# A new order for all elementwise instructions of a fused attention and two-layer kernel

## The chip, the cores and the metric

The kernel runs on one core of a Trainium2 chip. The metric is device time in microseconds (us), the median of several executions. Six queues matter here. PE is the matrix engine (PEld its weight loads), DVE is VectorE, ACT is ScalarE, POOL is GpSimd, and SP issues DMAs. Each engine works through its own instructions strictly in the order in which they were written, and waits on semaphores for what other engines have yet to deliver.

## The reference

Attention with a hash mask (a query sees only keys that fall into the same one of 64 buckets), then two feed-forward layers; the first uses mish, the second elu.

```
mask = q_bucket[:, :, :, None] == k_bucket[:, :, None, :]      # buckets: signs of q @ proj, k @ proj
scores = where(mask, scale * q @ k^T, -1e9)                    # 2 x 8 heads, 768 x 768, head size 64
attn = exp(scores - max) / (sum + 1e-9);  out = attn @ v
x = out as (1536, 512)
h = x @ w_in;  x = (h * tanh(softplus(h))) @ w_out             # 512 -> 2048 -> 512
h = x @ w_in2; x = where(h > 0, h, exp(h) - 1) @ w_out2        # 512 -> 2048 -> 512
```

Inputs are float32. Every factor is split into a rounded high part and a low part (names ending in hi and lo), and a product is the sum of three matmuls.

## The kernel before

**Attention** (to about 233 us). 16 heads of 6 query tiles each give 96 tiles. For a tile, PE computes scores `st` (L648), DVE takes the maximum while it copies them to `pt` (L651, L654), ACT does the exponential (L656). For a pair of tiles PE transposes `pt` into `tu` (L707, three pieces), ACT writes the high part `pth` (L712), DVE the low part `ptl` (L353, called from the split), and PE multiplies both with the values (`xt`, L720). There are two `tu` buffers, so a late `ptl` holds up the next transpose. POOL splits the inputs (`z`, `vt`) and divides and splits the finished heads (`xr`, L757, L761, then `x_hi` and `x_lo`).

**Weights.** 64 units of 128x512 float64 numbers come in by DMA and are turned into two float32 parts by `convert`, nine instructions each on ACT, DVE and POOL. The first three units are converted between the attention tiles; the DVE steps of these read and write SBUF alone (L405, L410, L413, L415, L418, with `wt` and `ws`). Later units keep one operand, `c`, in PSUM. Units 6 and 7, 10 and 11 and so on are pairs for which POOL also forms sums `sa` and `sb`.

**The two layers** (from about 233 us). `up` products give `h`, one per unit and column block; mish or elu makes `g` of it; `down` products of `g` are summed in `y_acc`. Pairs of units run as seven products with shared sums (a Strassen scheme, `pair_step`); for that `turn` forms differences of x first (`y_acc` as scratch, L1040, split into `T`), once before each layer's pairs. The last step of elu is the subtraction `g<-gg,g` (L353 through `elu`). It and the steps of `turn` may run on DVE or on POOL.

**What sets the order.** `Plan` collects all operations with their costs and dependencies, and `Plan.run` walks a simulated clock: for each engine it takes the waiting operation with the lowest priority number among those that can start soon, and of all engines the earliest start. That order is then emitted. Where an operation may run on DVE or POOL, the plan also decides which. In the plan, POOL and DVE operations marked `port` never overlap. The priority is the place in the program plus tables: `OFF` and `ODD` for attention (by kind of operation, and by kind and tile of the head), `SHIFT` for weights and layers. In the two layers PE's own order is fixed by the program; in attention PE's order comes from the tables too. `pool(n)` and `pool2(n)` are the plan's costs in ns for a POOL instruction over n columns.

Of the kernel before, what the change touches and what calls it, by code (L numbers as in the profile page):

```python
# [30 lines left out]
def unit_orders():  # L31
# [25 lines left out]
EDGE = {}  # L57
SHIFT = {
# [86 lines left out]
def pool(n):  # L145
    return 150 + 2.22 * n


def pool2(n):
    return 150 + 2.38 * n  # L150
# [144 lines left out]
def kernel(ctx, tc, qk, v, w, tab, out):  # L295
# [165 lines left out]
    def attention(p, ap, dp, pss, pst, psx, h_r):  # L461
# [52 lines left out]
        def order(i, name):  # L514
            return i + OFF[name] + ODD.get(name, (0,) * NQ)[i % NQ] + EDGE.get(f"{name}{i}", 0)

# [784 lines left out]
```

## Time and profile before

| | us |
|---|---|
| median of 3 runs | 739.52 (739.17 to 742.06) |
| profiled execution, its own time | 742.38 |
| its span, first to last instruction | 740.6 |
| PE busy in it | 727.1 |
| DVE, ACT, POOL busy | 579.4, 490.4, 423.2 |

[...] The profile's "idle before" of an instruction is the time its engine stood still just ahead of it, followed by what ended that.

### The profile page before, as it was taken

How to read it: one execution, taken by the hardware profiler on the slowest of the kernel's cores; microseconds unless marked ns; L12 is line 12 of the kernel's file. 1: busy time of each engine (PE TensorE's matmuls, PEld its weight loads, DVE VectorE, ACT ScalarE, POOL GpSimd, SP SyncE). 2: the span in 40 equal slices, each digit the busy share in tenths (PEclk: the TensorE clock that was granted, in tenths of full speed). 3: DMA queues.
4: the chain of work that ended last, by engine and by line, in shares of the span. 5: the costliest groups of instructions: out<-in, count | busy, mean ns of one | idle time of the engine just before them, and what ended most of it. 6: DMA issues, size and time to landing. Idle time of an engine off the chain costs nothing. (4 is left out here: it accounts for less than half of the span.)

```text
span 740.6 us, 11709 instructions
## 1 busy us (share of the span) xinstructions
PE 727.1 (98%) x4083; PEld 639.0 (86%) x4083; DVE 579.4 (78%) x1065; ACT 490.4 (66%) x977; POOL 423.2 (57%) x359
## 2 busy tenths in 40 slices
PE   8999999999999999999999999999999999999998
PEld 7999999999898887888888888887788888888887
DVE  6899999999998979486577668999766785866672
ACT  5998998989997666554273457467766754844740
POOL 5427735734637886446446536866664755765640
PEclk9999999999999999999999999999999999999999
DMA  6875867777620302122112202212121121121112
GB/s 191 206 187 150 204 176 178 190 175 184 143 61 29 114 30 70 44 86 85 58 58 74 98 30 86 86 57 81 34 86 58 58 86 58 58 85 58 58 72 99
DMA packets 27498, 72.93 MB, mean 98 GB/s; under 512 B 6048, under 2 KB 8240, under 8 KB 27440
## 3 DMA queue, kind: packets, MB, share of 16 engines
q1 hardware_dynamic: 27296, 72.17, 34.3%
q8 instruction: 32, 0.52, 0.3%
q14 instruction: 26, 0.21, 0.1%
q10 hardware_dynamic: 144, 0.01, 0.0%
HBM read 45.76 MB, written 3.19 MB: 66 GB/s over the span
## 5 line engine op out<-in xcount | busy, mean ns | idle before, releaser
L848 PE MATMUL h<-g,w 128*128 128x512 f32 x1140 | 267.1, 390 | 3.0 <-DVE g L353 3.0
L848 PEld LDWEIGHTS h<-g,w 128*128 128x128 f32 x1140 | 212.6, 188 | 48.0 <-DVE g L353 4.1
L353 DVE TENSOR_TENSOR ptl<-tu,pth 128x512 fp32r<-128x512 f32 x144 | 97.5, 687 | 7.4 <-ACT pth L712 5.0
L651 DVE TENSOR_SCALAR_CACHE_REDUCE pt<-st 128x768 f32<-128x768 f32 x96 | 90.6, 948 | 5.7 <-PE st L648 5.4
L656 ACT ACTIVATE pt<-pt,nb 128x768 f32<-128x768 f32 x96 | 90.7, 945 | 3.6 <-DVE nb L654 3.4
L712 ACT CAST pth<-tu 128x512 fp32r<-128x512 f32 x144 | 82.2, 582 | 13.6 <-PE tu L707 12.7
L707 PE MATMUL tu<-ident,pt 128*128 128x128 f32 x576 | 85.9, 275 | 2.9 <-DVE ptl L353 2.8
L353 POOL TENSOR_TENSOR wt<-wt,w 128x512 f32<-128x512 f32 x40 | 52.8, 1320 | 62.1 <-DVE c L415 39.4
L1202 DVE TENSOR_TENSOR y_acc<-h,y_acc 128x512 f32<-128x512 f32 x71 | 48.8, 687 | 50.3 <-PE h L848 50.2
L648 PE MATMUL st<-qkt 76*128 76x384 f32 (+1 forms) x384 | 86.7, 350 | 0.8 <-DVE pt L651 0.8
L720 PE MATMUL xt<-pth,vt 128*128 128x256 f32 x288 | 79.3, 304 | 0.0
L707 PEld LDWEIGHTS tu<-ident,pt 128*128 128x128 f32 x576 | 67.4, 140 | 10.4 <-DVE ptl L353 6.2
L720 PE MATMUL xt<-ptl,vt 128*128 128x256 f32 x288 | 72.7, 281 | 0.0
L648 PEld LDWEIGHTS st<-qkt 76*128 76x128 f32 (+1 forms) x384 | 63.8, 191 | 1.7 <-DVE pt L651 1.7
L848 PE MATMUL h<-x_hi,w 128*128 128x512 f32 x192 | 60.5, 390 | 0.0
L348 ACT CAST w<-wt 128x512 fp32r<-128x512 f32 (+1 forms) x64 | 37.2, 583 | 33.0 <-DVE wt L401 18.0
L423 POOL TENSOR_TENSOR wt<-wt,ws 128x512 f32<-128x512 f32 x24 | 31.9, 1328 | 42.5 <-DVE ws L418 42.0
L432 POOL TENSOR_TENSOR w<-wt,ws 128x512 fp32r<-128x512 f32 x40 | 53.4, 1335 | 4.6 <-DVE ws L418 2.2
L720 PEld LDWEIGHTS xt<-ptl,vt 128*128 128x128 f32 x288 | 54.7, 190 | 0.1
L720 PEld LDWEIGHTS xt<-pth,vt 128*128 128x128 f32 x288 | 54.4, 189 | 0.0
L398 DVE TENSOR_SCALAR c<-ws 128x512 int32<-128x512 int32 x61 | 42.0, 689 | 14.3 <-ACT ws L396 12.7
L350 POOL CAST z<-rw 128x768 fp32r<-128x768 f32 x14 | 11.6, 826 | 64.0 <-DMA qkt<-z 41.7
(151 smaller groups left out, 1549.8 us busy)
## 6 DMA issues: line engine op xcount, KB each, us to landing
wraw<-in_w_dram SPq DMA_DIRECT2D x64, 512.0 KB
qkt<-z SPq DMA_DIRECT2D x30, 384.0 KB
rw<-in_qk_dram SPq DMA_DIRECT2D x16, 384.0 KB
qkt<-z SPq DMA_DIRECT2D x31, 192.0 KB
vr<-in_v_dram SPq DMA_DIRECT2D x8, 384.0 KB
out_dram<-y_acc SPq DMA_DIRECT2D x11, 256.0 KB
rr<-dr SPq DMA_DIRECT2D x14, 192.0 KB
xs<-xr SPq DMA_DIRECT2D x14, 192.0 KB
```

The lines of the kernel that those rows point to most:

```text
L348: nc.scalar.copy(out=out, in_=in_)
L353: eng(e).tensor_tensor(out=out, in0=a, in1=b, op=ALU.subtract)
L398: o2 = p.op({DVE: dve(n)}, lambda e: nc.vector.tensor_scalar(out=bits(b), in0=bits(a), scalar1=3, scalar2=None, op0=ALU.logical_shift_left ...
L432: o9 = p.op({POOL: cost}, lambda e: nc.gpsimd.tensor_tensor(out=lo(), in0=t.tile, in1=s.tile, op=ALU.add), [o6, o8], [t, s, w_], prio)
L648: nc.tensor.matmul(st.tile[:, c, 0:HS], lhsT=wt.tile[0:n, q, t * 128:(t + 1) * 128], rhs=wt.tile[0:n, 2 + q, c * HS:(c + 1) * HS], start=( ...
L651: o = max_op = p.op({DVE: dve(S)}, lambda e: nc.vector.tensor_scalar(out=half(pt.tile), in0=st.tile[:, :, 0:HS], scalar1=-MASKED / SCALE, ...
L656: o = p.op({ACT: act(S, False) + 196}, lambda e: nc.scalar.activation(out=pt.tile, in_=pt.tile, func=AF.Exp, bias=nb.tile, scale=SCALE, ac ...
L707: nc.tensor.transpose(tu.tile[:, k, j], pt.tile[:, (2 * b + k) * 128:(2 * b + k + 1) * 128], ident)
L712: o = p.op({ACT: act(512)}, lambda e, tu=tu, ks=ks: nc.scalar.copy(out=hi.tile[:, ks], in_=flat(tu)), [o], [tu, hi], order(i, 'hi'))
L720: nc.tensor.matmul(xt.tile[:, 0:TH], lhsT=vt.tile[:, k, g % 2], rhs=m.tile[:, k], start=(k == 0 and j == 0), stop=(k == NKT - 1 and j == 1))
L848: nc.tensor.matmul(out(), lhsT=w_.tile[:, a, k], rhs=r, start=(start and n == 0), stop=(stop and n == 3 * len(ks) - 1), skip_group_check=True)
L1202: y = p.op({DVE: dve(n)}, lambda e, ya=ya, t=t, c=c: nc.vector.tensor_tensor(out=ya, in0=view(t.tile, c), in1=ya, op=ALU.add), [x, Y[m, c] ...
```

## The change

Only numbers change; no function but the two cost lines does. Both cost lines now say 140 + 2.185 n (1259 ns for 512 columns where they said 1287 and 1369). A third table, `EDGE`, which was empty, now shifts single operations of the first heads (1 to 5) and the last ones (13 to 15). All entries of `OFF`, `ODD` and `SHIFT` are new.

```diff
-EDGE = {}
+EDGE = {'rr5': -12.0, 'rh#1': -1.0, 'rh#2': -4.0, 'rh#3': 3.75, ...
 SHIFT = {
-    'P1#0': -28, 'P1#1': -25.25, 'P1.1': -5, 'P1c#0': -20.5, 'P1c#1': 3.5, 'P1c.1': -22.75, 'P2#0': 19.5,
...
+    'P1#0': -27.25, 'P1#1': -97.5, 'P1.1': 5.75, 'P1c#0': 114.75, 'P1c#1': 8, 'P1c.1': -51, 'P2#0': -17.5,
...
 def pool(n):
-    return 150 + 2.22 * n
+    return 140 + 2.185 * n
 def pool2(n):
-    return 150 + 2.38 * n
+    return 140 + 2.185 * n
```

What it does to the program: all lines of the kernel move down by two (L353 becomes L355). Every computation stays. 11 instructions go from DVE to POOL: 7 of the elu subtractions `g<-gg,g` (DVE 22 to 15, POOL 26 to 33), and of `turn` a net 4. PE's order is unchanged up to 20 us and in both layers; it changes around heads 2 to 4 and 13 to 15. In the middle of attention (heads 6 to 12) nearly all orders stay.

In the first heads, DVE's `wt0` step (L410 before, L412 now) comes ahead of the maximum of tile 23 and of one `ptl17`, three instructions earlier; on POOL the split of `z6` and the addition to `xr0` change places.

DVE, last heads, around `ws1`, a step in the conversion of weight unit 1 (`ptl79`, `ptl81`, `ptl83` are low parts; `pt85` and the like come from the maximum, `both15` is a mask). Before:

```order
L654 TENSOR_SCALAR nb83_3103<-mx83_3015 128x1
L415 TENSOR_SCALAR ws1_2827<-wt1_2872 128x512
L581 SCALAR_TENSOR_TENSOR both15_3096<-pj15_3080,both15_3096 64x384
L353 TENSOR_TENSOR ptl79_3078<-tu79_2_3090,pth79_3060 128x512
L651 TENSOR_SCALAR pt85_3127,mx85_3126<-st85_3098 128x768
```

Now:

```order
L355 TENSOR_TENSOR ptl79_3078<-tu79_1_3067,pth79_3059 128x512
L583 SCALAR_TENSOR_TENSOR both15_3099<-pj15_3080,both15_3099 64x384
L355 TENSOR_TENSOR ptl79_3078<-tu79_2_3091,pth79_3059 128x512
L653 TENSOR_SCALAR pt85_3126,mx85_3125<-st85_3103 128x768
L355 TENSOR_TENSOR ptl81_3144<-tu81_0_3112,pth81_3128 128x512
L653 TENSOR_SCALAR pt84_3155,mx84_3154<-st84_3120 128x768
L355 TENSOR_TENSOR ptl81_3144<-tu81_1_3130,pth81_3128 128x512
L656 TENSOR_SCALAR nb84_3175<-mx84_3154 128x1
L653 TENSOR_SCALAR pt87_3178,mx87_3177<-st87_3147 128x768
L355 TENSOR_TENSOR ptl81_3144<-tu81_2_3158,pth81_3128 128x512
L656 TENSOR_SCALAR nb87_3202<-mx87_3177 128x1
L656 TENSOR_SCALAR nb85_3204<-mx85_3125 128x1
L417 TENSOR_SCALAR ws1_2827<-wt1_2872 128x512
```

`ws1` stood between tiles' work ahead of the last `ptl79`; it now stands behind all of `ptl79` and `ptl81`, some 6 us of DVE work later.

ACT, first layer, around the first pair of units (`p6_01` and `p6_02` are copies of a PSUM bank that the next product waits for; `w8` and `w9` are high parts of weights). Before:

```order
L348 CAST w8_4078<-wt8_4075 128x512
L348 CAST T0_0_3697<-y_acc_3696 128x256
L348 COPY p6_01_4108<-h6_b1_4088 128x512
L348 CAST w9_4110<-wt9_4105 128x512
L348 CAST x_hi_64<-y_acc_3696 128x256
L348 COPY p6_02_4133<-h6_b1_4088 128x512
```

Now:

```order
L350 CAST w8_4104<-wt8_4088 128x512
L350 CAST T2_0_3701<-y_acc_3696 128x256
L350 COPY p6_01_4121<-h6_b1_4096 128x512
L350 CAST w9_4133<-wt9_4123 128x512
L892 ACTIVATE h6_b2_4110<-h6_b2_4110 128x512
L350 COPY p6_02_4146<-h6_b1_4096 128x512
```

The cast of `x_hi` out of `y_acc`, which needs a `turn` step of DVE, no longer stands ahead of `p6_02`. On DVE, the seven instructions that end with the step `wt9` had a `T` subtraction and a `y_acc` subtraction among them; now the steps of `w8` and `w9` follow each other up to `wt9` with none between.

POOL, start of the second layer. `g32` to `g35` are the first four elu outputs (the last figure is the column block), `w36` and `w37` the first `down` weights. Before:

```order
L353 TENSOR_TENSOR wt36_5978<-wt36_5978,w36_5982 128x512
L432 TENSOR_TENSOR w36_5982<-wt36_5978,ws36_5930 128x512
L353 TENSOR_TENSOR wt37_6077<-wt37_6077,w37_6081 128x512
L353 TENSOR_TENSOR g33_2_6102<-gg1217_6063,g33_2_6102 128x512
L353 TENSOR_TENSOR g32_1_6110<-gg1224_6075,g32_1_6110 128x512
L432 TENSOR_TENSOR w37_6081<-wt37_6077,ws37_6053 128x512
```

Now:

```order
L355 TENSOR_TENSOR T2_1_3702<-y_acc_3696,T2_1_3702 128x512
L355 TENSOR_TENSOR g33_2_6080<-gg1217_6051,g33_2_6080 128x512
L355 TENSOR_TENSOR wt36_6082<-wt36_6082,w36_6086 128x512
L434 TENSOR_TENSOR w37_6054<-wt37_6046,ws37_6025 128x512
L434 TENSOR_TENSOR w36_6086<-wt36_6082,ws36_6062 128x512
L1042 TENSOR_TENSOR y_acc_3696<-y_acc_3696 128x256
L355 TENSOR_TENSOR g35_0_6192<-gg1245_6162,g35_0_6192 128x512
L355 TENSOR_TENSOR T2_0_3701<-y_acc_3696,T2_0_3701 128x256
L355 TENSOR_TENSOR g34_2_6203<-gg1252_6186,g34_2_6203 128x512
```

`g35_0`, `g34_2`, `g32_2` and three `T` subtractions were DVE's and are POOL's now, `g32_1` went the other way, and `w36` comes behind `w37`.

## Rows read from the trace of the kernel before

**Rows 1.** The page: engines' busy time; costliest group (mean ns, idle, releaser).

```profile
PE 727.1 (98%) x4083; PEld 639.0 (86%) x4083; DVE 579.4 (78%) x1065; ACT 490.4 (66%) x977; POOL 423.2 (57%) x359
...
L848 PE MATMUL h<-g,w 128*128 128x512 f32 x1140 | 267.1, 390 | 3.0 <-DVE g L353 3.0
```

**Rows 2.** PE's waits, whole span: us in total, times, longest.

```profile
PE h L848 <- DVE g L353: 3.0, 3, 1.4
PE tu L707 <- DVE ptl L353: 2.8, 3, 1.0
...
PE h_b L848 <- ACT p L348: 0.8, 1, 0.8
...
PE st L648 <- DVE pt L651: 0.8, 2, 0.6
```

**Rows 3.** Windows: stretch, length, busy time by engine (instructions), clock, DMA.

```profile
60.00:180.00 120.00, 120.00 (x902) 116.45 (x901) 110.43 (x266) 110.16 (x245) 70.00 (x49) 1.00 0.73 179
...
720.00:741.00 21.00, 17.46 (x89) 14.76 (x87) 5.00 (x8) 0.00 (x0) 0.00 (x0) 1.00 0.28 100
```

**Rows 4.** Timeline at 55 us: start, length, engine, line, names, [idle <-releaser].

```profile
54.88 1.84 POOL L757 TENSOR_TENSOR xr<-xr,xs 128x768 f32<-128x768 f32 x1
...
55.27 2.00 DVE L410 SCALAR_TENSOR_TENSOR wt<-wraw,wt 128x512 int32<-128x512 int32 x1
...
57.93 0.66 PE L707 MATMUL tu<-ident,pt 128*128 128x128 f32 x4 [0.98 <-DVE ptl L353]
```

**Rows 5.** Timeline at 195 us.

```profile
194.47 1.84 POOL L353 TENSOR_TENSOR x_lo<-xr,x_hi 128x768 fp32r<-128x768 f32 x1
...
194.61 1.98 DVE L415 TENSOR_SCALAR ws<-wt 128x512 int32<-128x512 int32 x1
...
197.70 0.55 PE L707 MATMUL tu<-ident,pt 128*128 128x128 f32 x3 [1.04 <-DVE ptl L353]
```

**Rows 6.** Timeline, 280 to 299 us.

```profile
280.39 1.50 DVE L353 TENSOR_TENSOR T<-y_acc,T 128x256 fp32r<-128x256 f32 x1
...
282.52 0.62 ACT L348 CAST w<-wt 128x512 fp32r<-128x512 f32 x1 [2.30 <-DVE wt L401]
...
284.52 0.50 PE L848 MATMUL h_b<-x_hi,wb 128*128 128x512 f32 x1 [0.84 <-ACT p L348]
...
298.87 0.50 PE L848 MATMUL h<-g,w 128*128 128x512 f32 x1 [0.39 <-DVE g L353]
```

**Rows 7.** Timeline, 515 to 527 us.

```profile
515.92 2.36 DVE L353 TENSOR_TENSOR g<-gg,g 128x512 fp32r<-128x512 f32 x2
...
516.08 1.66 POOL L423 TENSOR_TENSOR wt<-wt,ws 128x512 f32<-128x512 f32 x1 [0.84 <-DVE ws L418]
...
518.34 5.75 PE L848 MATMUL h<-g,w 128*128 128x512 f32 x24 [1.29 <-DVE g L353]
...
523.04 2.35 DVE L353 TENSOR_TENSOR g<-gg,g 128x512 fp32r<-128x512 f32 x2
...
525.45 1.90 PE L848 MATMUL h<-g,w 128*128 128x512 f32 x7 [1.36 <-DVE g L353]
```

**Rows 8.** POOL and DVE groups by line and shape: count, busy us, mean ns, idle.

```profile
L353 POOL TENSOR_TENSOR g<-gg,g 128x512 fp32r<-128x512 f32 x26 | 33.5, 1298 | 14.6 <-ACT g L348 14.6
...
L1040 POOL TENSOR_TENSOR y_acc<-x_hi,x_lo 128x512 f32<-128x512 f32 x8 | 11.0, 1389 | 0.4 <-DVE x_lo L353 0.4
...
L1040 POOL TENSOR_TENSOR y_acc<-x_hi,x_lo 128x256 f32<-128x256 f32 x8 | 7.5, 952 | 0.0
...
L353 DVE TENSOR_TENSOR g<-gg,g 128x512 fp32r<-128x512 f32 x22 | 20.6, 954 | 3.1 <-ACT g L348 2.7
...
L353 DVE TENSOR_TENSOR g<-h_b,g 128x512 fp32r<-128x512 f32 x24 | 16.5, 686 | 7.6 <-ACT g L348 7.6
```

**Rows 9.** Timeline, 233 to 245 us.

```profile
233.08 0.47 PE L848 MATMUL h<-x_hi,w 128*128 128x512 f32 x1
...
236.16 0.67 ACT L396 ACTIVATE ws<-wraw 128x512 f32<-128x512 f32 x1
...
243.43 1.31 POOL L432 TENSOR_TENSOR w<-wt,ws 128x512 fp32r<-128x512 f32 x1
```

More of the change, by code (lines that the diff above doesn't have):

```diff
@@ L56 @@
 SEED, SPREAD = 0, 0.0
-EDGE = {}
+EDGE = {'rr5': -12.0, 'rh#1': -1.0, 'rh#2': -4.0, 'rh#3': 3.75, 'rh#13': -10.5, 'rh#14': 31.5, 'cp#1': 5.5, 'cp#3': 1.5, 'cp#14': -5.25, 'cp#15': 19.75, 'ld#1': -16.0, 'ld#2': -11.75, 'ld#13': -4.0, 'ld#14': 19.0, 'ld#15': 14.5, 'sp#1': -27.0, 'sp#2': -1.25, 'sp#13': -7.5, 'sp#14': -15.5, 'sp#15': -10.75, 'pj#2': -2.75, 'pj#3': -2.5, 'bits#2': -7.0, 'bits#3': -43.75, 'bits#13': 8.0, 'pc#2': 25.75, 'pc#3': 4.5, 'pc#13': 8.0, 'pc#14': -7.25, 'pc#15': -37.0, 'pb#1': -1.25, 'pb#2': 18.75, 'pb#3': 66.5, 'mk#1': 14.5, 'mk#2': 8.0, 'mk#3': 3.75, 'mk#13': -29.0, 'mk#14': 22.0, 'S0': 1.0, 'S1': 0.5, 'S2': 1.25, 'S4': 14.75, 'S6': -29.25, 'S7': -37.5, 'S8': -8.75, 'S9': -14.25, 'S10': -15.5, 'S87': -0.25, 'S88': 2.5, 'S90': 26.75, 'S91': 8.5, 'S92': -1.0, 'S94': 16.25, 'S95': 17.0, 'max0': -9.5, 'max1': 42.25, 'max2': 10.5, 'max3': -16.0, 'max5': -3.0, 'max6': 2.5, 'max7': -0.5, 'max8': 24.25, 'max9': 1.75, 'max10': -0.25, 'max11': -25.0, 'max12': -2.0, 'max84': -25.0, 'max85': 12.5, 'max86': 15.0, 'max87': -7.75, 'max88': 3.5, 'max89': -21.75, 'max93': -0.25, 'max94': -22.75, 'max95': 20.25, 'exp2': -1.75, 'exp3': -18.75, 'exp4': -8.5, 'exp5': -0.5, 'exp6': 14.5, 'exp7': 57.75, 'exp9': 2.0, 'exp10': 12.5, 'exp11': -3.0, 'exp12': -2.5, 'exp13': -11.25, 'exp86': -31.75, 'exp87': 4.0, 'exp88': -23.25, 'exp89': 3.0, 'exp90': 11.0, 'exp91': -0.25, 'exp92': -2.5, 'exp93': 7.0, 'exp94': 11.25, 'exp95': -11.0, 'sum5': -24.0, 'sum11': 1.5, 'sum87': 29.25, 'sum89': -7.0, 'sum93': 17.75, 'sum95': 6.5, 'eps5': -0.25, 'eps11': -4.75, 'eps85': -8.25, 'eps87': 14.75, 'eps89': -9.25, 'eps91': -20.25, 'eps93': -6.5, 'eps95': 48.0, 'T1': -12.75, 'T3': 10.75, 'T5': -29.75, 'T7': 28.75, 'T9': 7.75, 'T11': -8.0, 'T13': 1.0, 'T85': 8.75, 'T87': -21.75, 'T89': 8.5, 'T91': 8.0, 'T93': -0.5, 'T95': -11.5, 'hi3': 12.0, 'hi5': -0.25, 'hi7': 3.75, 'hi11': -63.0, 'hi13': -2.25, 'hi85': 21.25, 'hi87': 10.0, 'hi89': -10.25, 'hi91': 36.25, 'hi93': 4.25, 'hi95': 16.25, 'lo1': 3.75, 'lo3': -5.25, 'lo5': 13.5, 'lo7': 2.0, 'lo9': -8.75, 'lo11': -39.0, 'lo13': 4.0, 'lo85': -0.25, 'lo89': 27.25, 'lo91': -1.75, 'lo93': 17.0, 'lo95': -10.75, 'R91': -2.75, 'R93': -3.0, 'R95': 0.25, 'pv1': -4.25, 'pv11': 0.25, 'pv13': -0.25, 'pv85': 1.0, 'pv87': 11.5, 'pv91': 24.0, 'pv93': 11.75, 'pv95': 24.75, 'xc1': 19.0, 'xc3': -9.25, 'xc5': -52.75, 'xc7': -1.5, 'xc13': 3.75, 'xc85': -0.75, 'xc87': 42.75, 'xc89': -3.5, 'xc93': -0.5, 'xm5': -8.0, 'xm11': 8.0, 'rr11': 10.0, 'rh#15': 21.0, 'cp#2': 5.75, 'cp#13': 9.25, 'ld#3': -3.0, 'sp#3': 15.5, 'pj#1': -1.75, 'pj#13': 0.25, 'bits#1': -6.25, 'bits#14': 14.5, 'S13': -2.0, 'S86': 2.25, 'S89': 0.5, 'S93': 17.0, 'max4': 27.0, 'max91': -36.75, 'exp84': -2.0, 'sum85': 7.0, 'hi1': -16.25, 'hi9': -12.25, 'pv3': -1.75, 'pv5': -2.0, 'pv7': -0.25, 'pv9': 0.5, 'pv89': -28.25, 'xn11': 4.0}
@@ L131 @@
 WAIT = {'PE': 150, 'ACT': 0, 'DVE': 50, 'POOL': 50, 'SP': 100}
-OFF = {'rr': 41.5, 'rh': 63.5, 'cp': -137.25, 'ld': 2.0, 'sp': -1.25, 'pj': -5.75, 'bits': -149.5, 'pc': 18.0, 'pb': -54.0, 'mk': 208.25, 'v': 55.25, 'S': -1.5, 'max': -137.5, 'exp': 73.0, 'sum': 130.5, 'eps': 39.25, 'T': 11.25, 'hi': -16.75, 'lo': -121.5, 'R': 46.25, 'pv': 7.0, 'xc': 27.5, 'xa': -194.25, 'xn': -103.25, 'xh': -29.75, 'xm': 106.25}
-ODD = {'lo': [2.5, 0.0, 4.5, -89.5, 1.75, -25.0], 'T': [11.25, -11.5, 35.0, -11.25, 16.75, -10.0], 'pv': [7.25, -0.75, -0.5, -0.75, 16.0, -1.75], 'exp': [8.0, -86.0, -69.75, 0.25, -10.75, -1.0], 'hi': [-3.0, -2.0, 8.5, -1.0, -0.25, -7.5], 'S': [2.5, 1.25, 3.0, 0.0, 3.25, -1.25], 'xc': [2.75, -5.25, -4.25, -9.0, 0.0, 3.5], 'max': [1.75, 115.75, -2.0, 6.25, 6.0, 134.5]}
+OFF = {'rr': -9.0, 'rh': 17.75, 'cp': -38.25, 'ld': 7.5, 'sp': 0.75, 'pj': -5.75, 'bits': -198.5, 'pc': 91.0, 'pb': -170.0, 'mk': 182.25, 'v': -38.0, 'S': -1.0, 'max': -158.0, 'exp': 85.25, 'sum': 224.0, 'eps': -134.75, 'T': -51.25, 'hi': -10.25, 'lo': -225.25, 'R': 42.75, 'pv': 7.75, 'xc': 29.5, 'xa': 33.25, 'xn': -4.75, 'xh': -32.5, 'xm': -12.5}
+ODD = {'lo': [-18.0, 41.5, 21.5, -8.5, -9.25, 4.0], 'T': [-0.75, -36.5, -14.5, -7.0, 0.0, 14.5], 'pv': [0.0, 0.0, -4.25, -0.75, 0.0, -1.75], 'exp': [10.0, -81.0, -109.0, 33.25, -37.0, 43.25], 'hi': [2.0, 0.0, -98.75, 0.0, -4.25, 9.5], 'S': [2.5, 0.5, 3.5, 0.75, 2.5, -1.0], 'xc': [-0.5, 11.75, 2.0, -13.0, 6.0, -7.0], 'max': [-29.5, 1.0, -92.75, -2.0, 0.25, 0.0]}
 PE, ACT, DVE, POOL, SP = "PE", "ACT", "DVE", "POOL", "SP"
```

138 rows, old and new, of the table SHIFT are left out of this document.

## The prediction

> **What bounds the kernel now.** I read the busy times first, since they say how much there is to win: PE is busy for 727.1 of 740.6 us [rows 1], so 13.5 us is all that an order could give back if PE's own work stays, and it does (4083 matmuls before and now). Next come PE's waits, to see which part of the 13.5 us lies where the order changes [rows 2]. Then the windows: from 60 to 180 us PE has no idle time at all, and at the end 21.00 - 17.46 = 3.5 us is the closing chain (last addition and the store), whose order is unchanged [rows 3]. The timeline rows give the waits one by one: 0.98 us at 58 us [rows 4], 1.04 at 198 us [rows 5], 0.84 at 285 us and 0.39 at 299 us [rows 6], 1.29 at 518 us and 1.36 at 525 us [rows 7]. That is 5.90 us. The other waits in rows 2 belong to the first 20 us (0.8 us for `st`, and the third `tu` wait, 2.8 - 0.98 - 1.04 = 0.8); there neither PE's order nor its suppliers' changes, so they stay. A gap costs a little more than its idle time: a matmul lasts 390 ns but the next follows after 267.1 / 1140 = 234 ns [rows 1], so each gap also loses an overlap of 0.16 us. Six gaps then cost 5.90 + 6 x 0.16 = 6.9 us. That is the pool of this change.
>
> The reader should see why five of the six waits exist: DVE and POOL hinder each other. DVE's L410 took 2.00 us, running from 55.27 to 57.27, while POOL's L757 ran from 54.88 to 56.72 [rows 4]; L415 took 1.98 us beside POOL's `x_lo` [rows 5]; two `g` subtractions took 2.36 us beside POOL's L423, which itself took 1.66 us [rows 7]. The subtraction with one operand in PSUM takes 686 ns, the same one with both in SBUF averages 954 ns [rows 8]. The `ptl` or `g` that PE needs is queued on DVE behind, or is, such a slowed instruction.
>
> [...]
>
> **The change part by part.** *The `ws1` step (198 us).* It ran into POOL's `x_lo`. Now it stands some 6 us later on DVE, behind both remaining groups of low parts, and the `ptl79` that PE waited for stands ahead of it. POOL then reaches the addition `wt1`, which needs `ws1`, so POOL is more likely waiting for DVE than in its way. Gain between 0 (another POOL split is running) and 1.04 + 0.16 = 1.20; I take 1.2, because what PE waited for is now ahead of the slow step whatever POOL does.
>
> *The `wt0` step (58 us).* Three instructions earlier on DVE is about 1.3 us earlier by an order of one maximum and one low part (the low part as the 686 ns subtraction [rows 8]), so it starts near 54.0 rather than 55.27. POOL's addition began at 54.88 [rows 4]; in its place the `z6` split now stands, as long. The step then has about 0.9 us for its 0.69 us of work. Gain between 0 and 0.98 + 0.16 = 1.14; I take half, 0.6, since 0.2 us decides.
>
> *The bank copy `p6_02` (285 us).* ACT stood still for 2.30 us until DVE's `wt` step came, which was queued behind a `T` subtraction slowed to 1.50 us [rows 6], and then did a cast that waited for `turn` again. Now neither the subtraction nor the cast is ahead. Gain 0 to 0.84 + 0.16 = 1.0; I take 1.0, as two independent causes go. The 0.39 us wait 14 us later came from a `g` at DVE's end of a row of weight steps; bounds 0 and 0.55, I take 0.3.
>
> *The start of the second layer (518 and 525 us).* DVE's work from the last `y_acc` of the first layer to `g35_2` loses two weight steps, two 512-column and no 256-column `y_acc` steps, two of four large `T`, and three of nine `g`, against two more 256-column `T` and a larger `x_lo` in place of two small ones. The three `g` alone are 3 x 0.954 = 2.9 us [rows 8]; the rest at no less than 0.69 us each for six is 4.1, less some 1.1 us that comes back: about 6 us less on DVE. PE was 1.29 and 1.36 us late, together 2.65 + 2 x 0.16 = 3.0 us. What moved costs POOL 1.298 us per `g` [rows 8], and POOL has the later `g35_0` behind `w36`: the chain of `w36` on DVE stands 26 instructions ahead of `g35_2`, so it is early. Gain 0 to 3.0; I take 2.9.
>
> *The 11 instructions that go to POOL.* POOL is busy for 423.2 us of 740.6 [rows 1]; 11 more at 1.3 us at most are 14 us, hidden by PE as long as no result is late. Elsewhere in the second layer five more `g` (of blocks that PE needs later) go to POOL: each ends 1.298 - 0.954 = 0.34 us later by itself, and up to 1.3 us more if a weight step is ahead of it. Bounds for these: below, -0.5 (DVE is less hindered, but no PE wait stands in these stretches, so hardly a gain); above, 5 x 1.64 = 8 us. Rows 3 and the rest of rows 2 show no PE wait there at all, so there is slack; I take 0.5.
>
> *The turn from attention to the first layer.* POOL forms more sums for `turn` before it finishes weight `w3`: one more 512-column and four more 256-column sums, and one `T` less, 1.389 + 4 x 0.952 - 1.3 = 3.9 us [rows 8]. `w3` ended at 243.43 + 1.31 = 244.7, and PE needs it 66 matmuls after 233.08 [rows 9], at 233.08 + 66 x 0.234 = 248.5: 3.8 us of slack, plus what idle time POOL has there. ACT starts the `ws3` step after three mish steps and their casts instead of at 236.16 [rows 9]; these wait for the early products to end near 237.3, so it starts some 4 us later, and the rest of the chain took 8.6 us, of which two POOL instructions (2.6 us) are no longer between: it ends between 246.3 and 248.9. Cost 0 to 0.4 by this chain, to 1.5 with a hindered DVE step; I take 0.6. Four tiles of the last head are also exchanged, and a transpose follows its exponential closely; 0 to 1.0, I take 0.6.
>
> *Other orders.* Some 1500 rows of DVE and ACT queues differ in place. Where PE had no wait, a new one can only cost. By the nearest rows, one wait is 0.4 to 1.36 us and costs 0.16 more [rows 6, 7]; between 0 and four of them, I take half of one, 0.3.
>
> The sum: -(1.2 + 0.6 + 1.0 + 0.3 + 2.9) = -6.0, and +(0.5 + 0.6 + 0.6 + 0.3) = +2.0, together -4.0. Against the profiled execution that is 742.38 - 4.0 = 738.4. That execution lies 2.9 us above the median of the runs, 739.52; none of the waits can be put down to this difference, so I move the same difference to the median: **735.5 us**.
>
> **The rivals.** *The collisions only move* (within 0.5%). POOL has 14 us more to do, most of it reading SBUF, and the DVE steps that collide do not vanish; each collision taken away turns up elsewhere and half of them stop PE: 6.0 / 2 - 2.0 = 1.0 us gained, 738.5; if the gain is as above but the first-layer turn costs its 1.5 and the unforeseen four waits (4 x 0.9), -6.0 + 0.5 + 1.5 + 0.6 + 3.6 = +0.2, 739.7. For it: DVE is 110.43 of 120 us busy in attention [rows 3]. Against: four of the six waits have their cause removed from the queue ahead of what PE needs. That the new order does nothing for the time is this case too.
>
> [...]
>
> *POOL is late with its `g`* (slower). The mechanism: a `g` that DVE would finish in 0.954 us stands on POOL behind a weight step it does not need. Price: 7 `g` x (0.34 + 1.3) = 11.5 us if PE reaches each `down` product right when it would have been ready, against the 6.0 us gained: 739.5 + 5.5 = 745.0. It decides against the change from (6.0 + 3.7) / 1.64, six of the seven late. For it: PE already reached two of them early [rows 7]. Against: those two are the only ones.
>
> **How the numbers follow.** A difference of 0.5% (3.7 us, below 735.8 or above 743.2) is about what a measurement of this kernel can tell from none. The forecast has 0.55; its own range is 732.6 (every gain and no cost, 739.5 - 6.9) to 737, and 0.48 of it lies below 735.8, 0.07 above. The collisions that only move have 0.35, from 737 to 741. POOL late has 0.10, from 743.2 up. So faster is 0.48, the same 0.07 + 0.35 = 0.42, slower 0.10. The range goes from 732.6 to 740.0; it leaves out the late POOL and the top of the second case, some 0.05.
>
> **What would show it.** In the profile after, PE's busy time stays near 727 us and its waits behind 20 us fall from 5.9 to some 3 us. Right: no PE wait beside `ws1`, `p6_02`, `g35_0` and `g35_2`; the mean of DVE's `g<-gg,g` falls below 954 ns or their count alone falls. Wrong: a PE wait on `w3` near 248 us, on POOL's `g` in the second layer, or on `tu91`; or POOL's share rises with the same total of PE waits in other places. A startup that takes another time than before would make the sum wrong without any of these.

## The result, and the profile after the change

The changed kernel takes 743.69 us (median of 7 runs, 743.40 to 746.55) where the kernel before takes 740.87 (7 runs, 739.17 to 742.06). The ratio over all runs is 1.0052, 95% interval 1.0033 to 1.0071 (the two medians alone stand 0.4% apart): slower by about half a per cent, where 735.5 us and a range of 732.6 to 740.0 were forecast. The profiled execution took 746.55 us with a span of 744.7, against 742.38 and 740.6 before.

From the page and the groups by line, the rows that answer to [rows 1] and [rows 8] (all lines stand two lower now):

```profile
PE 730.6 (98%) x4083; PEld 641.4 (86%) x4083; DVE 573.2 (77%) x1054; ACT 487.5 (65%) x977; POOL 432.2 (58%) x370
...
L850 PE MATMUL h<-g,w 128*128 128x512 f32 x1140 | 266.4, 390 | 0.5 <-DVE g L355 0.5
...
L355 POOL TENSOR_TENSOR g<-gg,g 128x512 fp32r<-128x512 f32 x33 | 42.7, 1299 | 32.0 <-ACT g L350 31.7
...
L355 DVE TENSOR_TENSOR g<-gg,g 128x512 fp32r<-128x512 f32 x15 | 14.6, 980 | 3.3 <-ACT g L350 3.0
```

And PE's waits over the whole span, which answer to [rows 2]:

```profile
PE h_b L850 <- ACT p L350: 5.2, 2, 3.0
...
PE tu L709 <- DVE ptl L355: 0.8, 1, 0.8
...
PE h L850 <- DVE g L355: 0.5, 1, 0.5
```

The second list explains both halves of the result. What was to go has gone: the 3.0 us of waits for `g` are 0.5, and of the three waits for `ptl` only the one in the first 20 us is left. But a single kind of wait, for ACT's bank copies `p`, went from 0.8 us to 5.2, in two pieces. The first is in the first layer's first pair of units (6 and 7). The timeline there, with start, length, engine, and in brackets the idle time and what ended it:

```profile
278.07 0.68 ACT L398 ACTIVATE ws<-wraw 128x512 f32<-128x512 f32 x1 [0.51 <-POOL wa L355]
...
280.13 0.41 ACT L350 CAST T<-y_acc 128x256 fp32r<-128x256 f32 x1 [1.08 <-DVE y_acc L1042]
...
281.45 0.62 ACT L350 CAST w<-wt 128x512 fp32r<-128x512 f32 x1 [0.35 <-DVE wt L403]
281.98 0.40 ACT L350 CAST T<-y_acc 128x256 fp32r<-128x256 f32 x1
...
282.29 0.58 ACT L350 COPY p<-h_b 128x512 f32<-128x512 f32 x1
...
282.92 4.62 PE L850 MATMUL h_b<-T,wa 128*128 128x512 f32 x12 [2.19 <-ACT p L350]
```

The copy `p6_01` could have run once product 1 had filled the bank, near 279.4 us. It stands on ACT behind a cast of `T` that waited for DVE's `y_acc`, a weight step, the cast `w8` that waited for DVE's `wt`, and another `T`. PE stands for 2.19 us. The kernel before:

```profile
275.86 0.67 ACT L396 ACTIVATE ws<-wraw 128x512 f32<-128x512 f32 x1 [0.63 <-POOL wa L353]
...
279.63 0.59 ACT L348 COPY p<-h_b 128x512 f32<-128x512 f32 x1
...
280.79 2.88 PE L848 MATMUL h_b<-T,wa 128*128 128x512 f32 x12
```

There the weight steps `ws8`, `ws9`, `w8` and one `T` stood ahead of the copy as well. What is new is that `ws8` (the first row) begins 2.21 us later, with POOL's sum `wa6`, and that `x_hi` and a second cast of `T`, which waits 1.08 us, stand between. The same in the first pair (38 and 39) of the second layer, with what led to it:

```profile
516.98 1.30 POOL L355 TENSOR_TENSOR g<-gg,g 128x512 fp32r<-128x512 f32 x1 [6.43 <-ACT g L350]
...
529.12 0.62 ACT L350 CAST g<-gg 128x512 fp32r<-128x512 f32 x1 [2.74 <-DVE gg L902]
...
530.61 0.74 POOL L355 TENSOR_TENSOR w<-wt,w 128x256 fp32r<-128x256 f32 x1 [1.52 <-ACT w L350]
...
530.91 0.63 ACT L350 CAST wa<-sa 128x512 fp32r<-128x512 f32 x1
...
533.32 0.67 ACT L398 ACTIVATE ws<-wraw 128x512 f32<-128x512 f32 x1 [0.62 <-POOL wa L355]
...
538.58 0.62 ACT L350 CAST w<-wt 128x512 fp32r<-128x512 f32 x1 [1.45 <-DVE wt L403]
...
539.11 0.58 ACT L350 COPY p<-h_b 128x512 f32<-128x512 f32 x1
...
539.74 4.61 PE L850 MATMUL h_b<-T,wa 128*128 128x512 f32 x12 [2.98 <-ACT p L350]
```

Read from the bottom: PE waits for `p38_01`, which stands behind the cast `w41`, which waits for DVE's step of unit 41, which follows ACT's `ws40` and `ws41`, which wait until POOL has finished `wa38`. That was at 533.3 us; in the kernel before it was at 529.2. And `wa38` needs ACT's cast of the sum `sa38`, at 530.91 us, which stands behind the cast `g35_1`, and that waited 2.74 us for DVE. In the kernel before, `wa38` waited for that cast too, but `wa38` and `ws40` (the two rows below) began 4.1 and 3.8 us earlier:

```profile
527.88 1.29 POOL L353 TENSOR_TENSOR wa<-sa,wa 128x512 fp32r<-128x512 f32 x1 [1.89 <-ACT wa L348]
...
529.48 0.67 ACT L396 ACTIVATE ws<-wraw 128x512 f32<-128x512 f32 x1
```

The two last `PE` rows also show something that the wait alone does not explain: 12 matmuls take 4.62 us, where the same 12 took 2.88 in the kernel before (row of 280.79 us above). The windows (stretch, length, busy time and instructions by engine, granted clock, DMA share, GB/s):

```profile
280.00:283.00 3.00, 0.81 (x5) 0.35 (x3) 2.77 (x5) 2.38 (x5) 2.13 (x3) 1.00 0.00 0
283.00:287.50 4.50, 4.50 (x13) 3.53 (x14) 3.96 (x6) 2.67 (x5) 4.50 (x6) 0.62 0.34 117
...
536.00:540.00 4.00, 1.02 (x5) 0.56 (x4) 3.62 (x7) 2.23 (x5) 3.13 (x3) 1.00 0.37 131
540.00:544.00 4.00, 4.00 (x12) 3.10 (x12) 1.71 (x4) 2.71 (x5) 1.98 (x2) 0.58 0.35 131
```

Behind each wait the granted clock is about 0.6 over 4 us, that is, mostly at 0.50: it is 0.50 from 284 to 287 us and from 541 to 543 us, where matmuls come every 0.427 us, and 1.00 before and behind, where they come every 0.227. The account of the 4.1 us longer span: PE's waits behind 20 us are 6.8 us instead of 5.9 (+0.9), PE is busy for 730.6 us instead of 727.1 with the same matmuls (+3.5), and the start is 0.3 us shorter. Single runs show the second term coming and going: those with a mean granted clock of 0.995 took 745.3 to 746.6 us, those with 0.997 or 1.000 took 743.4 to 743.7. One part stays open: also these runs lie 2.5 to 2.8 us above the median of the kernel before, and the waits and the start give only 0.9 - 0.3 = 0.6. The profiled execution of the kernel before, with which this account compares, took 1.5 us more than that median, and no trace shows what the other runs had less of.

### The profile page after: what moved, and what is told of

Read it like the earlier page. It is cut to its first block, busy times and chain, and to the rows that moved or that the text cites. A ratio compares the mean times of both kernels' runs of the same rounds, so it can differ in the third digit from the quotient of the medians.

```text
span 744.7 us, 11707 instructions
## 1 busy us (share of the span) xinstructions
PE 730.6 (98%) x4083; PEld 641.4 (86%) x4083; DVE 573.2 (77%) x1054; ACT 487.5 (65%) x977; POOL 432.2 (58%) x370
## 5 line engine op out<-in xcount | busy, mean ns | idle before, releaser
L355 DVE TENSOR_TENSOR ptl<-tu,pth 128x512 fp32r<-128x512 f32 x144 | 96.8, 685 | 7.4 <-ACT pth L714 5.4
L355 POOL TENSOR_TENSOR wt<-wt,w 128x512 f32<-128x512 f32 x40 | 52.7, 1318 | 50.6 <-DVE c L417 18.4
L350 ACT CAST w<-wt 128x512 fp32r<-128x512 f32 (+1 forms) x64 | 37.2, 581 | 37.2 <-POOL wt L425 21.1
L355 POOL TENSOR_TENSOR g<-gg,g 128x512 fp32r<-128x512 f32 x33 | 42.7, 1299 | 32.0 <-ACT g L350 31.7
```

The lines of the kernel that those rows point to most:

```text
L350: nc.scalar.copy(out=out, in_=in_)
L355: eng(e).tensor_tensor(out=out, in0=a, in1=b, op=ALU.subtract)
```

## The experiments

Two of the kernels below have a few lines of code changed. The others let the plan run and then move named rows of an engine's queue, or put the layers' rows in the other kernel's order; nothing else of the order changes. They carry a helper ahead of the program, so that L350 is L414 there.

**The late copies moved forward.** First theory: the copies stand too far back on ACT, so move them. On ACT, both pairs:

```diff
 x_hi<-y_acc
+p6_01<-h6_b1
 T1_0<-y_acc
 ws9<-wraw9
 w8<-wt8
 T2_0<-y_acc
-p6_01<-h6_b1
 w9<-wt9
...
 w40<-wt40
+p38_01<-h38_b1
 y_acc<-h36_1
 y_acc<-h37_1
 w41<-wt41
-p38_01<-h38_b1
```

> The changed kernel with two rows moved and nothing else: on ACT the copy p6_01 goes four places forward (ahead of T1_0, ws9, w8 and T2_0), the copy p38_01 three places forward (ahead of two y_acc copies and w41). Theory A (the loss is these two copies, which stand behind casts that wait for DVE, and the half clock that follows each long wait): both PE waits on p (2.19 and 2.98 us idle, 2.35 and 3.14 us with the lost overlap) go, and the granted clock stays 1.0 behind them; 743.69 - 5.5 = 738.2 us, between 736.5 and 739.5, and no run above 740. Theory B (the waits only move: the casts that now come later stop PE instead): PE waits of some 2 us for w8, T2 or w41, 742 to 744 us. Theory C (the loss sits in attention or in POOL's g): under 1 us gained, 743 us.

> The changed kernel with only p6_01 moved four places forward on ACT. Theory A: the wait at 283 us goes, that at 540 us stays: 743.69 - 2.35 = 741.3 us, and the granted clock of 283 to 287.5 us is 1.0 instead of 0.62. If the two waits add, the gains of this run and of the one with p38_01 alone sum to that of both. Theory B: 743 us or more.

> The changed kernel with only p38_01 moved three places forward on ACT. Theory A: the wait at 540 us goes, that at 283 us stays: 743.69 - 3.14 = 740.5 us, granted clock of 540 to 544 us 1.0 instead of 0.58. Theory B: 743 us or more.

Measured: 746.16 us for both moves (ratio to the kernel before 1.0066, 1.0054 to 1.0078), 746.11 for pair 6 alone (1.0062, 1.0042 to 1.0081), 745.19 for pair 38 alone (1.0054, 1.0040 to 1.0068). None is better than the changed kernel; theory A fell in this form. With both moved, PE's waits and the timeline at the first pair:

```profile
PE h_b L914 <- ACT p L414: 5.6, 2, 2.8
```

```profile
283.56 0.69 DVE L1023 TENSOR_TENSOR h_b<-h_b,p 128x512 f32<-128x512 f32 x1
283.68 0.62 ACT L414 CAST w<-wt 128x512 fp32r<-128x512 f32 x1 [2.12 <-DVE wt L467]
...
284.78 0.59 ACT L414 COPY p<-h_b 128x512 f32<-128x512 f32 x1
...
285.43 0.50 PE L914 MATMUL h_b<-x_hi,wb 128*128 128x512 f32 x1 [2.81 <-ACT p L414]
```

The first copy is in time, and PE waits one product later for the second, `p6_02`, which is behind the cast `w9` (2.12 us idle for DVE's unit 9) and behind mish, which waits for an addition that DVE does after the unit-9 step. In pair 38 the same happens with `p38_02`, 2.78 us. So it is not one row: the whole chain of the pair (copy, addition, activation, copy) stands behind the weight steps of the next units on ACT and on DVE.

**Work for PE in the two waits.** Is the half clock a consequence of the wait? Product 2 gets its first matmul several times over, and the real one then overwrites the result:

```diff
+            for i in range(fill):        # 9 in pair 6, 12 in pair 38
+                nc.tensor.matmul(out(), lhsT=w_.tile[:, 0, ks[0]], rhs=rhs(0)[0], start=True,
+                                 stop=False, skip_group_check=True)
             for i, k in enumerate(ks):
```

> The changed kernel with useless work for PE in the two waits: the first matmul of product 2 is issued 9 times more in pair 6 and 12 times more in pair 38 (the real one then overwrites it), 9 x 0.227 = 2.0 us and 12 x 0.227 = 2.7 us; order and copies are as in the changed kernel. Theory A1 (the half clock of about 4 us behind each wait comes from PE's idle time there): the clock stays 1.0 in both stretches, each loses some 1.8 us less, and the runs at 745 to 746.5 us go: all within 743.0 to 744.2 us, profiled span 741.0 to 742.0 instead of 744.7. Theory A2 (the clock falls for a reason of its own): the stretches still show about 0.6, and runs above 745 us remain, or the time grows by up to 0.5 us where the filler is longer than the wait.

Measured: 743.01 us (742.30 to 744.00, 11 runs; 1.0028, 1.0020 to 1.0037). The windows of the same stretches:

```profile
283.00:287.50 4.50, 4.21 (x19) 3.12 (x18) 3.11 (x5) 3.17 (x7) 4.50 (x6) 1.00 0.52 167
...
540.00:544.00 4.00, 4.00 (x19) 3.21 (x18) 3.18 (x5) 2.71 (x6) 0.11 (x1) 1.00 0.21 81
```

With 21 more matmuls the kernel is not slower but, where the clock had fallen, faster: the runs above 744 us are gone, and the span of the profiled execution is 741.2 instead of 744.7 us. The clock fell because PE stood still, theory A1: with work in the wait it is 1.00 in both stretches, without it 0.62 and 0.58. The waits themselves (now of work instead of idling) still cost what they cost.

**The same two waits in the kernel before.** Its order stays; ACT writes the two copies several times, so that only they are late:

```diff
+                def run(e):
+                    for _ in range(EXTRA.get((u, i, part), 0)):     # 5 in pair 6, 7 in pair 38
+                        copy(e, low(k)(), bank(1)())
+                    return copy(e, low(k)(), bank(1)())
```

> The kernel before, in its own order, with two copies made late and nothing else: p6_01 is written 6 times in a row instead of once, p38_01 8 times, by ACT (about 0.53 us each, 2.65 and 3.7 us). PE then waits some 2.1 us ahead of the product on T in pair 6 and 3.1 us in pair 38. If such waits and the half clock behind them are what the changed kernel loses: granted clock near 0.6 in the 4 us behind each, as in the changed kernel, 741.2 + 2.1 + 3.1 + 2 x 0.16 = 746.7 us and up to 3.6 us more by the clock. If the clock in the changed kernel has another cause: 1.0 behind both waits, 746.7 us or less.

Measured: 747.59 us (746.95 to 750.03; 1.0085, 1.0061 to 1.0109).

```profile
281.02 4.60 PE L849 MATMUL h_b<-T,wa 128*128 128x512 f32 x12 [2.40 <-ACT p L349]
...
540.87 4.49 PE L849 MATMUL h_b<-T,wa 128*128 128x512 f32 x12 [3.64 <-ACT p L349]
```

```profile
540.00:544.00 4.00, 3.13 (x7) 2.49 (x8) 1.39 (x2) 2.18 (x5) 0.00 (x0) 0.58 0.00 0
```

The waits came out somewhat longer than expected (2.40 and 3.64 us), and the 0.84 us wait of [rows 6] disappeared behind the first. Two late copies alone, without any of the 1500 other moved rows, make the old kernel lose 6.2 us and show the same half clock.

**Each half of the change alone.** The layers' order of one kernel with the attention order of the other, row for row:

```diff
 attention: as changed      | attention: as before
-layers: as changed         |-layers: as before
+layers: as before          |+layers: as changed
```

> New order of attention, old order of the two layers, row for row: this part of the change alone. From the PE waits of the two traces, with their lost overlaps: attention from 20 to 232 us had 2.8 us before and has 2.5 after, and the start is 0.3 us shorter: 741.0 - 0.6 = 740.4 us, within 1 us. If attention's new order were what costs: 743 us.

> Old order of attention, new order of the two layers, row for row: the other part alone. PE waits and slow matmuls behind 232 us: 5.2 us before, 9.7 after, of these 3.6 by the half clock: 741.0 + 4.5 = 745.5 us where the clock falls, 742 where it does not; the two waits on the copies p stand where they stood. If the layers' new order gains what was predicted of it (3.9 us): 737 us.

Measured: new attention with old layers 741.94 us (1.0010, 0.9995 to 1.0025), no difference from the kernel before; old attention with new layers 743.73 us (1.0043, 1.0026 to 1.0060). So the loss is the layers'. The first half also shows where the attention's gain went. At its first pair:

```profile
276.00 0.66 ACT L462 ACTIVATE ws<-wraw 128x512 f32<-128x512 f32 x1 [0.62 <-POOL wa L419]
276.47 0.39 PE L914 MATMUL h_b<-x_hi,w 128*128 128x512 f32 x1
...
280.19 3.01 PE L914 MATMUL h_b<-T,wa 128*128 128x512 f32 x12 [0.84 <-ACT p L414]
...
284.63 0.50 PE L914 MATMUL h_b<-x_hi,wb 128*128 128x512 f32 x1 [1.42 <-ACT p L414]
```

PE reaches the pair 1.6 us earlier than before (276.47, not 278.07), but ACT's `ws8`, which waits for POOL's sums, does not (276.00, before 275.86). The 1.6 us come back as 0.84 us for the first copy and 0.58 us more for the second (1.42, was 0.84). With the old attention and the new layers the two waits for copies in pair 6 are 1.38 and 0.30 us; with both parts new, 2.19.

**POOL's queue ahead of pair 38.** On POOL the addition that unit 38 needs goes ahead of `T2_0` and `g34_2`, and the low half of `w39`, which waited for ACT, goes back:

```diff
 g35_0<-gg
+wt38<-wt38,ws38
 T2_0<-y_acc,T2_0
 g34_2<-gg
-wt38<-wt38,ws38
...
-w39<-wt39,w39
 sb38<-wt38,sa38
 wa38<-sa38,wa38
 wb38<-sb38,wb38
+w39<-wt39,w39
```

> The changed kernel with two rows moved on POOL, second layer alone: the addition wt38 two places forward, behind g35_0 but ahead of T2_0 and g34_2, and the low half of w39, which waited 1.52 us for ACT, three places back, behind wa38 and wb38. ACT and DVE keep the changed order. Theory F (what makes pair 38's copies late is POOL: its sums for pair 38 end at 533.3 us, 529.2 us before the change, and the weight steps 40 and 41 wait for them): wa38 ends some 3 us earlier, ws40 too, the wait of 2.98 us at 540 us falls to 0.5 us or less, that at 283 us stays at 2.2; 743.69 - 3 = 740.6 us. Rival (the order of ACT and DVE alone decides): the wait at 540 us stays above 2 us, time as the changed kernel.

Measured: 744.90 us (1.0055, 1.0040 to 1.0071). The wait at 540 us is gone, but not for the reason that theory F gave:

```profile
517.42 1.30 POOL L489 TENSOR_TENSOR wt<-wt,ws 128x512 f32<-128x512 f32 x1 [0.48 <-DVE ws L484]
...
519.38 1.30 POOL L419 TENSOR_TENSOR g<-gg,g 128x512 fp32r<-128x512 f32 x1
...
520.71 0.60 ACT L962 ACTIVATE gg<-h 128x512 f32<-128x512 f32 x1 [1.70 <-POOL g L419]
...
526.16 8.03 PE L914 MATMUL h<-g,w 128*128 128x512 f32 x22 [2.62 <-DVE g L419]
...
529.62 0.62 ACT L414 CAST g<-gg 128x512 fp32r<-128x512 f32 x1 [2.16 <-DVE gg L966]
...
532.11 1.30 POOL L419 TENSOR_TENSOR wa<-sa,wa 128x512 fp32r<-128x512 f32 x1 [2.53 <-ACT wa L414]
```

`g34_2` is late now; ACT's next elu waits 1.70 us for its buffer, the `g` behind it are late, and PE stands for 2.62 us at 526 instead, with the half clock behind that too (0.50 from 526 to 532 us). `wa38` ended no earlier than in the changed kernel; PE only came later. POOL had its other sums ready by 529.6 us and then stood 2.53 us for ACT's cast, which is behind the cast `g35_1`, and that waited for DVE. So theory F fell in its form: the order of POOL alone makes the `g` late and does not bring `wa38` forward, since the queues of ACT and DVE hold it too. Nor does the wait of 2 us or more that the rival forecast at 540 us show.

**The whole chain of the pair ahead.** What can wait is then the weights of the *next* units. On ACT and DVE:

```diff
 ACT x_hi<-y_acc
+ACT p6_01<-h6_b1
 ACT T1_0<-y_acc
 ACT ws9<-wraw9
 ACT w8<-wt8
 ACT T2_0<-y_acc
-ACT p6_01<-h6_b1
-ACT w9<-wt9
-ACT h6_b2<-h6_b2
 ACT p6_02<-h6_b1
+ACT h6_b2<-h6_b2
 ACT g6_0<-h6_b2
+ACT w9<-wt9
+DVE h6_b2<-h6_b2,p6_01
 DVE c9<-ws9
 DVE wt9<-wraw9,c9
-DVE h6_b2<-h6_b2,p6_01
```

and likewise `p38_01`, `p38_02` and DVE's addition ahead of `w41` and the steps of unit 41.

> The changed kernel with the whole first pair of both layers put ahead of the next pair's weights: on ACT p6_01 and p6_02 (p38_01 and p38_02) go ahead of the cast w9 (w41), which now comes behind g6_0 (g38_0); on DVE the addition h6_b2 <- p6_01 (h38_b2 <- p38_01) goes ahead of the weight steps 9 (41). Theory D (after p_first: the whole chain of the pair stands behind weight steps on ACT and DVE, and taking one copy forward only lets the next one be late): both long PE waits go at last, PE waits from 232 us on fall from 5.7 to about 0.6 us (the 525 us one stays), the granted clock stays 1.0, time 743.69 - 5.5 = 738.2 us. Theory E (the weights themselves are late by then, whatever the order): PE waits for w8 or w40 instead, or 2 to 3 us later at the next pair, 742 us or more.

Measured: 741.36 us (738.37 to 742.64; 1.0004, 0.9990 to 1.0017). The first pair is cured but for 0.33 us; pair 38 has a third copy, and that one was late now:

```profile
541.49 0.66 ACT L462 ACTIVATE ws<-wraw 128x512 f32<-128x512 f32 x1 [2.17 <-POOL w L498]
542.05 0.57 ACT L414 COPY p<-h_b 128x512 f32<-128x512 f32 x1
...
542.67 2.71 PE L914 MATMUL h_b<-T,w 128*128 128x512 f32 x6 [2.39 <-ACT p L414]
```

Moving it ahead of `ws42` and `ws43` as well:

```diff
 w41<-wt41
+p38_01<-h38_b1
 ws42<-wraw42
 ws43<-wraw43
-p38_01<-h38_b1
```

> As chain_first, and the third copy of pair 38 (the second p38_01) goes on ACT ahead of the weight steps ws42 and ws43, of which ws43 waited 2.17 us for POOL's w41. If nothing else is late behind it, the wait of 2.39 us at 542.67 us and the half clock behind it go: the profiled span falls from 740.9 by 2.4 + 0.2 + 1.7 to 736.6 us, the time from 741.4 to about 737.5 us (736.5 to 739), which is below the kernel before by 0.3 to 0.6%. If the loss moves on again, a wait of 2 us appears at ws42, ws43 or w41 and the time stays at 740 us or more.

And two more rows at the start of the second layer:

```diff
+DVE g35_2<-gg,g35_2
 DVE x_lo<-y_acc,x_hi
-DVE g35_2<-gg,g35_2
...
+ACT w39<-wt39
 ACT g35_1<-gg
 ACT y_acc<-h
-ACT w39<-wt39
```

> As chain_all, with two more rows moved at the start of the second layer: on DVE g35_2 ahead of the x_lo before it (PE waits 0.52 us for it at 522 to 525 us), and on ACT the cast w39 two places forward, ahead of the cast g35_1 that waits 2.74 us for DVE, since POOL stands still 1.52 us for w39 ahead of its sums for pair 38. Expected: the 0.52 us wait goes to 0.1, wa38 ends 1.5 us earlier; 0.5 us less than chain_all. If POOL's earlier work meets DVE's g: no gain, or a wait on g of 0.5 to 1.5 us.

Measured: 737.58 us (736.53 to 738.92; ratio 0.9944, 0.9924 to 0.9964) and, with the two further moves, 737.95 (0.9947, 0.9930 to 0.9965). The first is faster than both kernels. Its busy row of the page, PE's two waits in the layers, and the two products that had waited:

```profile
PE 726.4 (99%) x4083; PEld 637.9 (87%) x4083; DVE 572.5 (78%) x1054; ACT 486.6 (66%) x977; POOL 432.5 (59%) x370
```

```profile
PE h L914 <- DVE g L419: 0.5, 1, 0.5
PE h L914 <- POOL w L498: 0.3, 1, 0.3
```

```profile
279.69 2.88 PE L914 MATMUL h_b<-T,wa 128*128 128x512 f32 x12
...
532.49 3.01 PE L914 MATMUL h_b<-T,wa 128*128 128x512 f32 x12
```

No wait for a copy is left, and none for `w9`, `w41` or the units behind, but for 0.33 us at 284.7 us for a weight from POOL (unit 8, by its place in the queue): these weights had the slack that the copies lacked. The figures close: 737.58 plus the two waits of the changed kernel with their lost overlaps (2.35 and 3.14) is 743.07 us; the kernel with the filled waits, which has the waits' length without the half clock, measures 743.01. The second kernel took the 0.5 us wait for `g35_2` away and got 0.33 and 0.23 us for the next `g` in its place: nothing gained. Nor did `wa38` end 1.5 us earlier (529.2 us, 529.1 without the moves), though POOL no longer waited for `w39`: ACT's cast for it still stands behind `g35_1`, which now waited 3.58 us.

## Why the prediction was wrong, step by step

- *`ws1` and `wt0`*: right as far as they went. There is no wait at 198 us, and 0.07 us at 58, though the `wt0` step is still slowed (1.33 us beside POOL's split). Wrong was that the 1.8 us taken for them were added to the sum as if they reached the end (the waits that went, with their overlaps, are 2.3 us). The half with the new attention alone shows that they do not: PE came to the first pair 1.6 us earlier and waited there for the copies. The prediction did not ask "what is late next" for this term. Rows 4 and 5 show slowed steps, 2.00 and 1.98 us beside POOL's, where the same two lines took at most 0.72 and 0.43 us for the other two of the first three units; by what mechanism no run shows.
- *The bank copy `p6_02`*: this step failed, with its sign. I looked at what no longer stands ahead of `p6_02`, and not at `p6_01`, in the same block of the order three rows above. It stands behind `T1_0`, `ws9`, `w8` and `T2_0`, and these came late, because `ws8` waited for a sum of POOL that ended 2.2 us later and `T1_0` for DVE. The wait for `p6_02` did go (-1.0), but 2.35 us came just ahead of it: +1.35 in all. And `p6_02` itself would have been 2.81 us late, as moving `p6_01` alone showed, since "neither is ahead" overlooked that `w9` still is and mish now is, with DVE's addition behind the unit-9 step. The 0.39 us `g` wait at 299 us went as assumed.
- *The start of the second layer*: the waits for `g` fell as forecast, 1.29 + 1.36 us to 0.52 (2.9 was taken, 2.3 came). But the check on the cost stopped at `w36`. POOL's sums for pair 38 ended 4.1 us later, and the pair's first copy, which stands behind unit 41 as it did before, came late with them: +3.14 us. Two things were late together there: `sa38` on POOL, behind the `g` that had moved to it (ready at 529.1 us, 524.9 before), and ACT's cast of it, behind `g35_1`, which waited for DVE.
- *The 11 instructions to POOL*: no PE wait on any `g` of POOL, so the 0.5 taken for one did not come, and POOL's busy time rose by 9.0 us, not 14; what they cost lies in the weights of the item above. The rival "POOL late with its `g`" had the place right and the order reversed: not a `g` behind a weight step, but weight steps behind `g35_0` and `g34_2` (POOL stood still 6.43 us for the first, but `wt38`, put right behind it, still had to wait 0.48 us for DVE). Turned round, as POOL's other order showed, the `g` are what is late.
- *The turn to the first layer*: no wait on `w3` (taken 0.6). Last heads: five waits of 0.08 to 0.35 us between 190 and 228 us, together 1.0, none of them on `tu91`; taken 0.6.
- *Other orders*: the mis-sized term. I bounded one unforeseen wait by the waits that the old trace happened to show (0.4 to 1.36 us) and took half of one. The two real ones were 2.19 and 2.98 us, and behind waits of this length lay a cost that no row of before could show: the half clock, 3.5 us in the profiled run.
- *The sum*: with the pair's chains in front, 737.58 against 741.44 us in the same comparison, -3.9 us, and -4.7 in the profiled spans; the forecast was -4.0. That the two agree is in part luck: since the row moves also removed other waits in pair 6, this does not confirm each term; it shows that gains of about the size assumed were there to be had. What was missing were two waits of +5.5 us together and the clock. The base was low as well: the median that the forecast started from, 739.52 us over three runs, is 740.87 over seven, 1.35 of the 8.2 us by which the forecast missed.
- *The rival "the collisions only move"* came nearest in its account: POOL's share rose and the total of PE's waits stayed, in other places (6.8 for 5.9 us). Its mechanism was not it. DVE's `g` average 980 ns where they took 954 [rows 8], and what PE waited for was not a slowed instruction but a short one behind late work in its queue.

What stays open: why the 0.84 us wait of the old order, and not a longer one, was all that the old layers had with the old attention is clear only in outline (weights, copies and PE arrived nearly together there); which of DVE's and POOL's moves makes pair 6's sums end 2.2 to 2.4 us later was not tried row by row; and for pair 38 no run has made POOL's `sa38` and the cast `g35_1` early separately.

## What to carry to other kernels

When an order is changed, follow every row of which PE waits in the new order, not only those on which it waited in the old one; the rows to check first are short copies that free a buffer and stand in one queue behind work for something needed later. A gain upstream counts only up to the next thing that does not come earlier with it. And a longer stop of PE has to be priced with the slow stretch that may follow it (here 1.6 to 2.9 us behind waits of 2.2 to 3.64 us).

## What the runs showed of the hardware

The matrix engine's granted clock fell from 1.00 to 0.50 after waits in the middle of a busy kernel. In the profiled executions all waits between 2.2 and 3.64 us behind the start were followed, at once or up to 1.3 us after the wait's end, by a stretch at 0.50 in which matmuls came every 0.427 us instead of 0.227 (for the runs with one pair's copy moved only the mean clock of 0.995, the same as in the changed kernel, says so); behind the waits of 1.29 and 1.36 us [rows 7] and of 1.42 us (new attention, old layers) the clock stayed at 1.00. Such a stretch lasted some 3.4 us, an estimate from the mean clock of 0.62 over 4.5 us in the changed kernel; behind the 2.62 us wait of POOL's other order the clock was 0.50 for the whole 6 us from 526 to 532 us. Behind four of these waits 12 matmuls took 4.49 to 4.62 us, where they took 2.88 without a wait, so 1.6 to 1.7 us more. Behind the 2.62 us wait 22 matmuls took 8.03 us, 2.9 us more than the 21 x 0.227 + 0.39 = 5.2 estimated from the spacing at 1.00. That is from 44% of the wait (3.64 us) to a little over all of it. The fall does not come in every execution: two of the seven of the changed kernel had a mean clock of 1.000 (how long their waits were is not on record). Filling the wait with matmuls whose result is thrown away kept the clock at 1.00 and took the runs of 745.3 to 746.6 us away.
